# A new table of edits to the issue order of a two-layer attention and mixer kernel: the set-up and some thirty later instructions change places

## The chip, the core and the metric

The kernel runs on one core of a Trainium2 chip. The metric is device microseconds of one execution. Lower is better. The core's engines each take their own list of instructions in order and meet only through semaphores: TensorE (PE, with its weight loads PEld), ScalarE (ACT), VectorE (DVE), GpSimd (POOL), and SyncE (SP), which issues the transfers.

## The reference

The input x has 2048 rows (tokens) of 448 values. Two layers are applied, each an attention block A and a mixer block B, all with the same weights.

```python
x = x + A(layernorm(x)); x = x + B(layernorm(x))      # twice
# A: qkv = x @ wqkv, 16 heads of 28; softmax(q k^T * 28**-0.5) v; then @ wo
# B: h = gelu(layernorm(x) @ w1), shifted by rows in four column groups, @ w2; x1 = x + that
#    x1 + gelu(layernorm(x1) @ w3) @ w4
```

## The kernel before, in words

**Staging.** The rows are 16 tiles of 128. The 16 heads stand in four groups of four, and each head is padded from 28 to 32, so that one group fills 128 partitions. Keys are kept as kT (four groups by columns of tokens), queries as qT, values as vaug (token tiles by padded heads). The scores of one head and one key tile against 512 queries are one matmul with 32 rows (L1646). They go to PSUM banks 0 to 4: one ACT instruction (L1884) takes the exponentials of three banks (128x1536), the next of the two others (128x1024), in turn, and writes them to the ring PT of 15 slots. While ACT works on one set of banks, PE fills the other. The products with the values (L1042, 128x32 a piece) add up in bank 5. Banks 6 and 7 serve all other matmuls: the projections of keys, queries and values, the mixer's layers, and fillers, which are matmuls of the identity (L2377) that only keep PE at work. A part of the exponentials is computed by DVE instead (L1728 to L1762).

**Set-up.** Rows 0 to 511 are loaded, normalised on DVE (L1236, L1237, L1251, with the reciprocal root on POOL, L1244), transposed on PE in 16 pieces of 128x128 (L1275, four to a tile, each tile in a bank of its own) and copied to xT by DVE (L1282). Meanwhile ACT packs the key weights into wk_pad in four copies (L1180), squares their first 128 rows (L1192, into a slot of PT), packs two pieces of the query weights into wq_pad (L1180; POOL packs the other two, L1185) and squares their first 128 rows (L1192, into fb). PE sums the columns of these squares: four one-column matmuls for the keys and four for the queries (L1042 by the helper mm; ps<-ones_bf,PT and ps<-ones_bf,fb). DVE copies the eight sums to csum (L1204), PE adds them up by head (ps<-csum,astat), and DVE and POOL turn the two into a ratio for each head (L1206 to L1215, with a power on POOL, L1210). The first key projection (L1051 by the helper mm4; four steps ps<-xT,wk_pad over the four pieces of 128 features) goes to bank 7. ACT squares it (L1381) and adds a constant into kT (L1399); PE sums the squares by head (ps<-sq,astat), DVE takes the maximum (L1411), and from it and the ratio come the biases of the queries (L1560, L1562). With them ACT writes the first qT (L1459, from bank 5), and the first scores and exponentials can start.

**Order.** A planner in the kernel makes a list of 11,186 operations, numbered in the order in which it placed them (an operation is one instruction, or four matmuls side by side where the helper mm4 or a filler issues it). Then a method rearranges it by two tables that were written out beforehand:

```python
        for (a, b) in moves:
            p, q = prv[a], nxt[a]
            nxt[p] = q
            if q is not None:
                prv[q] = p
        for (a, b) in moves:
            q = nxt[b]
            nxt[b], prv[a], nxt[a] = a, b, q
```

MOVES holds pairs (a, b): operation a is taken out of its engine's list and put right behind operation b. WEAVE holds one letter an operation (t PE, s ACT, v DVE, g POOL, d SP) and says in which order over all engines the operations are noted. From that order each operation's waits are worked out: for data that it reads, for buffers that it overwrites. On the chip only the order within an engine and these waits count.

Of the kernel before, what the change touches and what calls it, by code (L numbers as in the profile page):

```python
# [61 lines left out]
)  # L62
WEAVE = (
    "vdvvvvsgdvgvvdtgtvgdtvtgdtsgtgvdvtvttdvtvvtdttvtvdgtgtdvtvtdtstvvtdgsvtttdtsgtttttstttsvttttvstttttgtvttstttvt",
    "tgsvtttvtttvvttttvvtvvtvtvtvtvtstgtstsvtttvvtvvtvvtsttvvtsvvtttstvttstvttvvtgtsvtttvvstvttsvttvtttsvtttvttsttv",
    "svtgvgvvtttsvttttvttttvttvdstvttttttvttsvttvttttvstvtdttvtttvtvtdsttttvtstttttdvtstvtdtttttvtttttstvdttttvvstt",
    "vtvsttttttvvtvgdtgtttsvvtttttttvtsvgtttgvtttttsvtdtttgttvtdtttsvtdttvttdtvtdstvtdvttttsvtgtttttttvtstttttgttts",
    "vttttdvstttvtgsvtttvtttttttvtdsvttdtttdtsttvttdtgtsttvttttttstvttttttgtvtstvtdtttstvttttttttgttsttttttsttvtvtg",
    "tsttvttvtttvsvttvtvttttvttstttvtsvdtttdtvtdvtttttvsdvtvtttdvsdvttvtdttdtvtsvtvdtttvvtstvtttvtttttttsttttttttts",
    "vtttvtttvstdttttvtgttstttvtttttsvtttttvstttvtttvttttsttvttttttsvttvtvtvtvtvsttvtvststtvdtttttgtttdvtstttttttvs",  # L70
    "tttttttttdtgsvtttttttsvgttttdtgdvsttdtvtgstvttttttttttsttttttsttvtttgtsttvttttttstvttgttttvstttvttdtsdttvttttt",
    "ttvsttttvtttsttvttvtvtvvtvsttttvvtsvtvttvtttttttvsttttvttsttvtvttstvtdttdtvsttttttttvtgtttstttttstttttttttttst",
    "vtttttgsvttvddsvtttdvtvtdtttsvtttttvtvvvvsvtttvtvvsvtvttvtvttvttvttvsttttvttsvttgttttvtdtsdvttttdvsttvtttttttt",
# [57 lines left out]
    "tdttvtttsvttttdttvttttttstvttttttvstvttttvttvtsttttvdsttvtdgtttttttttsttttttvsttvttvtdttttvsdttttvttttttstttvt",  # L131
    "tttttvttsdtvttttvttdtstdvtttvtdstvttdtttvstttttgttttttttstttvtttvtstttvttttttdsvttttttttvsgttdttttdvtsttvtttts",
# [18 lines left out]
    "tsttgttttvttttttdgtvttgtsvtttttttgtvstttttttgttttvtgttttgttvsttdtttvtttstvtttttttttttttsdvttttttttttttvsttttvt",  # L151
# [9 lines left out]
    "tvtgttgstvttttttvtttttttttttvdtstttgtvttttstttttvttttttttttttsvtttttttttttttvstttvtttttttsttttttsttttttttttttt",  # L161
# [2320 lines left out]
```

## Time and profile before

| what | value |
|---|---|
| median of 3 runs | 1025.42 us (1025.31 to 1028.83) |
| profiled execution, its own time | 1025.07 us |
| its span, first to last instruction | 1023.4 us |
| granted TensorE clock over the span | 1.000 |
| start of the first exponential (L1884) | 15.97 us |
| exponential of 128x1536 | x375, mean 1553 ns |
| exponential of 128x1024 | x406, mean 1130 ns |

The span is 1.7 us shorter than the profiled execution's own time. "x8" behind a line of the timeline is the number of instructions merged in it; the first column is the start, the second how long they took together. "[0.90 <-DVE bc L1562]" says that the engine stood idle for 0.90 us before, and what ended it. Where nothing holds them up, the exponentials of the trace start 1.33 us (128x1536) and 0.90 us (128x1024) after one another, less than their means: the spans shown overlap.

### The profile page before, as it was taken

How to read it: one execution, taken by the hardware profiler on the slowest of the kernel's cores; microseconds unless marked ns; L12 is line 12 of the kernel's file. 1: busy time of each engine (PE TensorE's matmuls, PEld its weight loads, DVE VectorE, ACT ScalarE, POOL GpSimd, SP SyncE). 2: the span in 40 equal slices, each digit the busy share in tenths (PEclk: the TensorE clock that was granted, in tenths of full speed). 3: DMA queues.
4: the chain of work that ended last, by engine and by line, in shares of the span. 5: the costliest groups of instructions: out<-in, count | busy, mean ns of one | idle time of the engine just before them, and what ended most of it. 6: DMA issues, size and time to landing. Idle time of an engine off the chain costs nothing.

```text
span 1023.4 us, 35818 instructions
## 1 busy us (share of the span) xinstructions
PE 969.9 (95%) x16109; PEld 408.7 (40%) x16109; DVE 813.1 (79%) x1572; ACT 981.0 (96%) x894; POOL 291.4 (28%) x462
## 2 busy tenths in 40 slices
PE   8999999999999999999999999999999999999998
PEld 4332443443333243333433443433433433444565
DVE  8877999989888958876877868688898589866651
ACT  8999999999999999999999999999999999999942
POOL 3312021531353006252425112012624120532230
PEclk9999999999999999999999999999999999999999
DMA  4643412310321014122141124423301020121101
GB/s 126 155 108 116 127 45 80 53 39 23 75 62 28 12 37 96 23 48 33 45 114 33 38 68 135 141 75 91 64 25 38 18 68 13 34 56 32 26 12 34
DMA packets 99393, 62.55 MB, mean 61 GB/s; under 512 B 68712, under 2 KB 88552, under 8 KB 99240
## 3 DMA queue, kind: packets, MB, share of 16 engines
q1 hardware_dynamic: 99240, 60.27, 23.0%
q8 instruction: 126, 2.06, 0.8%
q14 instruction: 27, 0.22, 0.1%
HBM read 28.16 MB, written 16.76 MB: 44 GB/s over the span
## 4 chain that ended last, share of the span: by engine, by line
ACT 71%; PE 23%; DVE 3%; DMA 1%; issue 1%; SPq 0%; DVEq 0%; ACTq 0%
ACT PT L1884 65%; PE ps L1051 13%; PE ps L1646 5%; PE ps L1042 4%; ACT h2T L2331 2%; ACT fb L2150 1%; PE ps L2377 1%; ACT L1884 1%; DVE h2T L2309 0%; ACT hT L2132 0%; DMA rT<-ub 0%; ACT L2331 0%; DMA PT<-in_A_wqkv_dram 0%; DMA obf<-in_A_x_dram 0%; DMA rscr<-rT 0%
## 5 line engine op out<-in xcount | busy, mean ns | idle before, releaser
L1884 ACT ACTIVATE PT<-ps 128x1024 bf16<-128x1024 f32 (+1 forms) x782 | 887.4, 1332 | 3.5 <-PE ps L1646 2.2
L1646 PE MATMUL ps<-qT,kT 32*128 32x512 bf16 (+1 forms) x2304 | 269.9, 335 | 24.2 <-ACT PT L1884 17.9
L1042 PE MATMUL ps<-PT,vaug 128*32 128x512 bf16 (+1 forms) x2420 | 245.9, 341 | 0.9 <-DVE vaug L1488 0.2
L1051 PE MATMUL ps<-xT,w 128*32 128x512 bf16 (+4 forms) x2656 | 178.1, 344 | 4.2 <-DVE h2T L2309 3.0
L1646 PEld LDWEIGHTS ps<-qT,kT 32*128 32x128 bf16 x2304 | 69.8, 91 | 256.0 <-ACT PT L1884 227.4
L2377 PE MATMUL ps<-ident 128*32 128x256 bf16 x3348 | 145.9, 277 | 2.0 <-POOL ident L1136 1.5
L1042 PEld LDWEIGHTS ps<-PT,vaug 128*32 128x32 bf16 x2420 | 74.0, 95 | 89.5 <-issue 70.9
L2377 PEld LDWEIGHTS ps<-ident 128*32 128x32 bf16 x3348 | 94.8, 97 | 28.9 <-issue 12.1
L1991 POOL TENSOR_TENSOR otn<-ub,fb 128x512 bf16<-128x512 f32 (+1 forms) x31 | 35.4, 1141 | 211.4 <-DMA fb<-rscr 211.4
L1728 DVE TENSOR_SCALAR yd<-ps 128x512 int32<-128x512 f32 x109 | 74.5, 684 | 22.5 <-PE ps L1646 21.0
L1051 PEld LDWEIGHTS ps<-xT,w 128*32 128x32 bf16 (+1 forms) x2656 | 69.5, 95 | 56.0 <-issue 22.9
L1051 PE MATMUL ps<-w,h2T 128*32 128x448 bf16 x1120 | 75.4, 355 | 4.4 <-ACT h2T L2331 4.3
L1755 DVE SCALAR_TENSOR_TENSOR fb<-yd 128x512 f32<-128x512 uint16 x109 | 79.0, 728 | 0.7
L1757 DVE SCALAR_TENSOR_TENSOR fb<-fb,yd 128x512 f32<-128x512 f32 x109 | 78.3, 721 | 0.7
L1762 DVE SCALAR_TENSOR_TENSOR PD<-yd,PD 128x512 int16<-128x512 int16 x109 | 75.0, 690 | 1.6
L2309 DVE CAST h2T<-ps 128x512 bf16<-128x512 f32 (+1 forms) x70 | 44.4, 635 | 16.0 <-PE ps L1051 14.9
L1384 POOL TENSOR_TENSOR sq<-qT 128x512 bf16<-128x512 bf16 x24 | 28.5, 1188 | 95.8 <-DVE qT L1443 93.0
L1384 POOL TENSOR_TENSOR sq<-kT 128x512 bf16<-128x512 bf16 (+2 forms) x32 | 30.3, 949 | 83.1 <-DVE kT L1398 80.0
L1759 DVE TENSOR_SCALAR PD<-fb 128x512 bf16<-128x512 f32 x109 | 51.5, 475 | 1.0
L1051 PE MATMUL ps<-xT,wk_pad 128*32 128x512 bf16 (+2 forms) x576 | 47.5, 359 | 0.9 <-issue 0.3
L1646 PE MATMUL ps<-wk_pad,kT 32*128 32x512 bf16 x256 | 39.6, 384 | 4.5 <-ACT PT L1884 4.0
L1051 PE MATMUL ps<-xT,wq_pad 128*32 128x512 bf16 x512 | 43.2, 382 | 0.1
(189 smaller groups left out, 1194.6 us busy)
## 6 DMA issues: line engine op xcount, KB each, us to landing
uscr<-ub SPq DMA_DIRECT2D x28, 256.0 KB
ub<-uscr SPq DMA_DIRECT2D x28, 256.0 KB, 6.8
fb<-rscr SPq DMA_DIRECT2D x24, 256.0 KB
xnd<-xn SPq DMA_DIRECT2D x28, 128.0 KB, 2.0
xd<-x_res SPq DMA_DIRECT2D x16, 224.0 KB, 2.2
x_res<-xd SPq DMA_DIRECT2D x16, 224.0 KB, 4.2
w<-in_B_w_dram SPq DMA_DIRECT2D x5, 448.0 KB, 6.0
obf<-in_A_x_dram SPq DMA_DIRECT2D x16, 112.0 KB
```

Of the source, the lines that this page charges most:

```text
L1042: return lambda e: e.matmul(out=out, lhsT=lhsT, rhs=rhs, start=start, stop=stop, **kw)
L1051: r.append(e.matmul(out=out[c:c + w, :], lhsT=lhsT[:, c:c + w], rhs=rhs, start=start, stop=stop, tile_position=(0, c)))
L1384: return both("sq", 0.15 + NW * 0.0018, 0.07 + NW * 0.00104, lambda e: e.tensor_tensor(out=sq[:, si, 0:NW], in0=src, in1=src, op=ALU.mult) ...
L1646: yield op("pe", (0.005 + NW * 0.00042) / nc_, lambda e, i=i, kc=kc, j=j, g=g, qt=qt, a=a, NW=NW, bank=bank: e.matmul(out=ps[:, bank, i * ...
L1728: yield op("dve", c_ps(512), lambda e: e.tensor_scalar(out=y, in0=ps[:, bi(bank), :], scalar1=SCALE * L2E * FS, scalar2=-126.0 * FS, op0=A ...
L1755: yield op(D_[0][0], D_[0][1], lambda e: e.scalar_tensor_tensor(out=q, in0=lo, scalar=E2 / E3 * FS, in1=lo, op0=ALU.add, op1=ALU.mult), re ...
L1757: yield op(D_[1][0], D_[1][1], lambda e: e.scalar_tensor_tensor(out=q, in0=q, scalar=E1 / E3 * FS * FS, in1=lo, op0=ALU.add, op1=ALU.mult) ...
L1759: yield op(D_[2][0], D_[2][1], lambda e: e.tensor_scalar(out=pdt, in0=q, scalar1=E3 / FS ** 3, scalar2=E0, op0=ALU.mult, op1=ALU.add), rea ...
L1762: yield op(D_[3][0], D_[3][1], lambda e: e.scalar_tensor_tensor(out=pdt.bitcast(I16), in0=hi, scalar=128.0, in1=pdt.bitcast(I16), op0=ALU. ...
L1884: yield op("act", 0.069 + n * w * 0.000833, lambda e, bk=bk, s0=s0, n=n, w=w: e.activation(out=PT[:, s0:s0 + n, 0:w], in_=ps[:, bk[0]:bk[0 ...
L2309: ev = op("dve", c_ps(m * NW), lambda e, hr=hr, pv=pv: e.tensor_copy(out=hr, in_=pv), reads=[("ps", bi(b))], writes=hk, touch=[b])
L2377: return [e.matmul(out=ps[32 * c:32 * c + 32, bi(b), 0:256].rearrange("p (a n) -> p a n", n=128), lhsT=ident[:, 32 * c:32 * c + 32], rhs=i ...
```

## The change

Forty-one pairs are added to MOVES and six taken out; WEAVE is adapted. No operation is added or taken away, and no operation computes anything else. The lists of SP and POOL keep their order. The core of the diff, with all added pairs in whole lines of it:

```diff
@@ -17,60 +17,64 @@
...
-    (241, 247), (243, 241), (274, 285), (276, 274), (555, 550), (572, 568), (574, 572), (564, 575), (565, 564),
-    (595, 587), (597, 595), (604, 638), (605, 604), (606, 605), (652, 648), (657, 655), (756, 745), (758, 756),
...
+    (94, 115), (95, 94), (96, 95), (97, 96), (125, 118), (128, 125), (130, 134), (238, 231), (244, 238), (245, 244),
+    (246, 245), (247, 246), (261, 266), (262, 261), (274, 285), (276, 274), (555, 550), (572, 568), (574, 572),
+    (564, 575), (565, 564), (595, 587), (597, 595), (599, 597), (601, 599), (603, 601), (604, 634), (605, 604),
+    (606, 605), (645, 606), (646, 645), (647, 646), (648, 647), (652, 643), (657, 655), (756, 745), (758, 756),
+    (759, 758), (856, 850), (857, 856), (858, 857), (930, 935), (931, 930), (937, 931), (913, 941), (916, 913),
+    (966, 951), (964, 981), (965, 964), (975, 987), (1024, 1018), (1026, 1024), (1031, 1026), (991, 1031),
...
+    (7286, 7288), (7300, 7306), (7301, 7300), (7302, 7309), (7338, 7334), (7500, 7488), (7472, 7493), (7473, 7472),
...
-    (9616, 9627), (9680, 9672), (9681, 9680), (9682, 9681), (9684, 9682), (9697, 9689), (9699, 9697), (9700, 9699),
...
+    (9616, 9626), (9627, 9642), (9680, 9672), (9681, 9680), (9682, 9681), (9684, 9682), (9697, 9689), (9699, 9697),
...
+    (10134, 10128), (10135, 10134), (10597, 10591), (10675, 10653), (10676, 10675), (10677, 10676), (10683, 10663),
...
+    (11181, 11180), (107, 92), (4484, 4523), (5925, 5889), (6339, 6324), (7096, 7213), (8003, 7983), (8678, 8674),
+    (242, 232), (560, 593), (727, 732), (746, 762), (914, 904), (912, 907), (1033, 1011), (1041, 1037), (1453, 1431),
...
+    (5678, 5657), (5912, 5878), (5951, 5905), (6131, 6120), (6329, 6322), (6473, 6500), (7298, 7283), (7393, 7379),
+    (7406, 7393), (7434, 7390), (7466, 7424), (7450, 7445), (7791, 7769), (7991, 7973), (8016, 7987), (8032, 8016),
...
 WEAVE = (
-    "vdvvvvsgdvgvvdtgtvgdtvtgdtsgtgvdvtvttdvtvvtdttvtvdgtgtdvtvtdtstvvtdgsvtttdtsgtttttstttsvttttvstttttgtvttstttvt",
...
+    "vdvvvvsgdvgvvdtgtvgdtvtgdtsgtgvdvtvttdvtvvtdttvtvdgtgtdvtvtdtstvvtdgsvtttdtsgtttttstttsvttttvstgtttttttvtttttt",
...
```

In words, with the planner's numbers:

- Set-up, PE: the four column sums of the key weights (94 to 97) stood after the first transpose of the third tile (91) and ahead of the seven last transposes (99 to 108); now they stand behind the third of six fillers that follow the transposes (115). The first two steps of the key projection (125, 128) move ahead of the four column sums of the query weights (119 to 123). The sum by head (130, ps<-csum,astat) moves from between the second and third step of the key projection to behind the fourth (134).
- Set-up, ACT: the square of the query weights (107) moves ahead of the second copy into wq_pad (93).
- Near 23 to 26 us of the trace, PE: the last step of a value projection (238) and four products with the values (244 to 247) move ahead of three score matmuls (233 to 235) and a sum of key squares (237); three scores (264 to 266) move ahead of two steps of a query projection (261, 262). DVE: the copy of the second value tile (242) moves up by two places.
- Near 55 to 63 us: three scores (599, 601, 603) move ahead of five products with the values; two scores (640, 641) and two steps of a value projection (638, 643) move behind four products (645 to 648); a bias on DVE (560) moves back by seven places.
- Near 90 to 100 us, PE: two steps of a key projection (913, 916) move back by 19 places, past seven scores; two products (964, 965) back by ten; one step of a key projection (991) back by 18.
- Near 683 to 692 us: two products (7472, 7473) move back by some 15 places, one step of a query projection (7500) up by seven, and on DVE a step of its own exponentials (7393, L1759) up by three, another (7466, L1755) up by four, and the last step of a query group (7450, L1472) up by one.
- Near 885 us: the product 9627 moves back past six mixer steps (9616 to 9642) and six scores. Near 963 us: the product 10683 moves up by eleven.

More of the change, by code (lines that the diff above doesn't have):

```diff
@@ L45 @@
     (9149, 9148), (9150, 9149), (9317, 9307), (9312, 9339), (9313, 9312), (9315, 9313), (9316, 9315), (9414, 9403),
[16 rows of a table removed]
[17 rows of a table added]
 )
 WEAVE = (
-    "vdvvvvsgdvgvvdtgtvgdtvtgdtsgtgvdvtvttdvtvvtdttvtvdgtgtdvtvtdtstvvtdgsvtttdtsgtttttstttsvttttvstttttgtvttstttvt",
-    "tgsvtttvtttvvttttvvtvvtvtvtvtvtstgtstsvtttvvtvvtvvtsttvvtsvvtttstvttstvttvvtgtsvtttvvstvttsvttvtttsvtttvttsttv",
-    "svtgvgvvtttsvttttvttttvttvdstvttttttvttsvttvttttvstvtdttvtttvtvtdsttttvtstttttdvtstvtdtttttvtttttstvdttttvvstt",
-    "vtvsttttttvvtvgdtgtttsvvtttttttvtsvgtttgvtttttsvtdtttgttvtdtttsvtdttvttdtvtdstvtdvttttsvtgtttttttvtstttttgttts",
+    "vdvvvvsgdvgvvdtgtvgdtvtgdtsgtgvdvtvttdvtvvtdttvtvdgtgtdvtvtdtstvvtdgsvtttdtsgtttttstttsvttttvstgtttttttvtttttt",
+    "ttttvgssvvttttttttvvvvvvtvvvtvtstgtstsvtttvvtvvtvvtsttvvtsvvtttstvttstvttvvtgtsvtttvvstvttsvttvtttsvtttvttsttv",
+    "svtgvgvvtttstvtttttvtttstvttvttvtdttttsvtvttvttsvttvtdttvtttvttvdstttttvstttttdvtstvtdtttttvtttttstvdttttvvstt",
+    "vtsvttttttvvtvgtdtgttsvvtttttttvtsvtgttgvtttttsvttdttgttvttdttsvtdttvttdtvtdstvtdvttttsvtgtttttttvtstttttgttts",
     "vttttdvstttvtgsvtttvtttttttvtdsvttdtttdtsttvttdtgtsttvttttttstvttttttgtvtstvtdtttstvttttttttgttsttttttsttvtvtg",
-    "tsttvttvtttvsvttvtvttttvttstttvtsvdtttdtvtdvtttttvsdvtvtttdvsdvttvtdttdtvtsvtvdtttvvtstvtttvtttttttsttttttttts",
-    "vtttvtttvstdttttvtgttstttvtttttsvtttttvstttvtttvttttsttvttttttsvttvtvtvtvtvsttvtvststtvdtttttgtttdvtstttttttvs",
+    "tsttvttvtttvstvttvttttvttstttvtsvdtttdtvtvdvvsdvtvtttdttttvtsdvttvtdttdtvtsvtvdtttvtvtsttttvtttvttttstttttttts",
+    "vtttvtttvstdttttvtgtttstvttttttsvtttttvstttvtttvttttsttvttttttsvtvttvtvtvvtsttvtvststtvdtttttgtttdvtstttttttvs",
     "tttttttttdtgsvtttttttsvgttttdtgdvsttdtvtgstvttttttttttsttttttsttvtttgtsttvttttttstvttgttttvstttvttdtsdttvttttt",
-    "ttvsttttvtttsttvttvtvtvvtvsttttvvtsvtvttvtttttttvsttttvttsttvtvttstvtdttdtvsttttttttvtgtttstttttstttttttttttst",
-    "vtttttgsvttvddsvtttdvtvtdtttsvtttttvtvvvvsvtttvtvvsvtvttvtvttvttvttvsttttvttsvttgttttvtdtsdvttttdvsttvtttttttt",
+    "ttvsttttvtttsttvttvtvtvvtvstttvvsvtvttvtttttttvsttttvttsttvtttvttstvttdttdvsttttttttvtgttsttttstttttttttttsttt",
+    "vtttvstgttvddsvtdtvttvdttttsvttttvtvttvvvsvtttvtvvsvtvttvtvttvttvttvsttttvttsvttgttttvtdtsdvttttdvsttvtttttttt",
     "tvttsvttdvttvvtvtdvsvttvdttvtttttdttttvsttsttvsttttttvttsttttvttvtttsvttttvtttsttttttvttttttttvtsttttvtttstvtt",
@@ L130 @@
     "vttttttvgttttdtstttdtvtttsttttvtttttdvtvsttttvttttstttttttvtttttvsttttvtttsvtttvdtttttstttvtttttsvttttvgttvdst",
-    "tdttvtttsvttttdttvttttttstvttttttvstvttttvttvtsttttvdsttvtdgtttttttttsttttttvsttvttvtdttttvsdttttvttttttstttvt",
-    "tttttvttsdtvttttvttdtstdvtttvtdstvttdtttvstttttgttttttttstttvtttvtstttvttttttdsvttttttttvsgttdttttdvtsttvtttts",
+    "tdttvtttsvttttvdttttttvttstttvttttsvttvttttvttstttvtdsdvttgttttttttttsvttttttvsttvtttttvttvsdttttvttdttstttttt",
+    "vttttdtvsttvtdttttttdstttvtttvdstvttdtttvstttttgttttttttstttvttttvstttvttttttdsvttttttttvsgttdttttdvtsttvtttts",
     "vdgtttvtdttsttvttttttsttgtttttttsttvttsvgttttttttvtstvtttttsdvttttttvttsvtttvtdttsttvtvttsvdtttttvdtstttvttttv",
@@ L150 @@
     "ttttgttvtgtvsttttgtttttdtvgsgtttvtttgtvtttgtstdvtttttttgvgttsvttttdtttgttttvttttttttttttgtsvtttttttdgtttvttttt",
-    "tsttgttttvttttttdgtvttgtsvtttttttgtvstttttttgttttvtgttttgttvsttdtttvtttstvtttttttttttttsdvttttttttttttvsttttvt",
+    "tsttgttttvttttttdgtvttgtsvtttttttgtvstttttttgttttvtgtttgttvsttdtttvtttstvttttttttttttttsdvttttttttttttvsttttvt",
     "ttttttvttsttttvttttttttttstvtvtttdtgtttttstttttttvttttttttttttstvttvttttttvtttttvtttvtdtvttttttvtttttvttttdttv",
@@ L160 @@
     "tdvtttttttttttttstttttttttttttstvtttttvtttsvtvttttgttgvttttttsttttttvtttttttttstttvtttttvsttttvttdgtttvtvtsttt",
-    "tvtgttgstvttttttvtttttttttttvdtstttgtvttttstttttvttttttttttttsvtttttttttttttvstttvtttttttsttttttsttttttttttttt",
+    "tvtgtttgstvttttttvttttttttttvdtsttttgvttttstttttvttttttttttttsvtttttttttttttvstttvtttttttstttttttstttttttttttt",
     "tttvttttttttvstttttvtttsttttvtttttvtttttvttttsvtttttvtttsttvtvtgttgttsgtttttgttvstgtvttgttttgtttgttgvttvgtgtgt",
```

64 rows, old and new, of the table MOVES are left out of this document.

## The prediction

> **What bounds the kernel now.** First the page: busy shares, and the chain of work that ended last.
>
> ```profile
> PE 969.9 (95%) x16109; PEld 408.7 (40%) x16109; DVE 813.1 (79%) x1572; ACT 981.0 (96%) x894; POOL 291.4 (28%) x462
> ACT 71%; PE 23%; DVE 3%; DMA 1%; issue 1%; SPq 0%; DVEq 0%; ACTq 0%
> ```
>
> ACT is idle for 42 us in all. Next, what ACT waited for, from the first exponential to the start of the tail (16 to 970 us):
>
> ```profile
> ACT PT L1884 <- PE ps L1646: 2.2, 4, 0.7
> ACT fb L2150 <- DVE fb L2149: 0.8, 1, 0.8
> ACT PT L1884 <- PE ps L1042: 0.3, 1, 0.3
> ```
>
> The columns are the total, the number of waits, the longest. Only 3.3 us in 954 are real waits. So an edit in this stretch can gain little, and the time before the first exponential counts in full, because an unbroken ACT list moves with it. The timeline of the set-up:
>
> ```profile
> 8.15 0.61 ACT L1192 ACTIVATE PT<-wk_pad 128x512 bf16<-128x512 bf16 x1
> 8.82 0.25 PE L1042 MATMUL ps<-ones_bf,PT 128*128 128x1 bf16 x4 [0.66 <-ACT PT L1192]
> 8.94 0.55 PE L1275 MATMUL ps<-ident,xn 128*128 128x128 bf16 x7
> 9.30 0.76 DVE L1282 COPY xT<-ps 128x512 bf16<-128x512 bf16 x2 [0.76 <-PE ps L1275]
> 9.61 0.61 ACT L1192 ACTIVATE fb<-wq_pad 128x512 bf16<-128x512 bf16 x1
> 10.46 0.61 PE L1051 MATMUL ps<-xT,wk_pad 128*32 128x512 bf16 x8
> 11.12 0.61 PE L1051 MATMUL ps<-xT,wk_pad 128*32 128x512 bf16 x8
> 11.79 0.60 ACT L1381 ACTIVATE sq<-ps 128x512 bf16<-128x512 f32 x1 [1.56 <-PE ps L1051]
> 12.97 0.69 DVE L1411 TENSOR_REDUCE kmaxc<-ps 128x1 f32<-128x512 f32 x1 [1.01 <-PE ps L1051]
> 14.34 0.78 ACT L1459 ACTIVATE qT<-ps,bc,rcol 128x512 bf16<-128x512 f32 x1 [0.90 <-DVE bc L1562]
> 15.97 2.37 ACT L1884 ACTIVATE PT<-ps 128x1536 bf16<-128x1536 f32 x2
> ```
>
> Seven ready transposes stand behind column sums that wait 0.66 us for ACT; DVE waits 0.76 us for them, and the delay goes down the key chain to the exponential. Last, PE's waits (24 to 105 us) and its fillers, from windows restricted to the identity:
>
> ```profile
> PEld ps L1646 <- ACT PT L1884: 25.1, 61, 1.1
> PE ps L1646 <- ACT PT L1884: 2.1, 5, 0.8
> 45.00:55.00 10.00, 0.00 (x0) 0.00 (x0) 0.00 (x0) 0.00 (x0) 1.00 0.44 118
> ```
>
> There is not one filler from 45 to 95 us: PE has no spare work to drop there. Its waits are for banks that ACT still reads. PE and ACT bound this stretch together, and what counts is by how much both move.
>
> **The change part by part.** The sum is made against the profiled execution, 1025.07 us (span 1023.4 and 1.7 around it). The median is 0.35 above it.
>
> Set-up. The first transpose of the third tile starts at 7.93 and the others follow it 0.055 apart, where they now start at 8.94. The third tile's last starts at 8.10, not 9.05. The trace has 0.255 from that start to DVE's copy, so 8.35; but DVE's earlier two copies started at 7.79 and 8.13 and copies follow 0.34 apart, so the third copy starts at 8.46 and the fourth at 8.80, ending at 9.22 instead of 10.06. Three fillers fit before the moved sums, which still start at 8.82 with the ACT square; three more fillers of 0.11 and the mode change of 0.15 end near 9.39. There the key projection starts, 1.07 earlier than 10.46.
>
> Its first two steps take 0.23 each, to 9.84. The query sums then need ACT's query square. That square now follows the copy that it reads, so it can't overlap it: the trace has such a pair at L1163 and L1165 (end 3.51, next start 3.54), against 0.095 of overlap between independent copies. It starts at 9.235 + 0.03 and ends 0.61 later, at 9.88, instead of 10.22. The sums start at 9.94 (0.06 behind, as at 8.82), last 0.18 to the next step, and steps three and four start at 10.12 and 10.35. The fourth ends 0.39 later, at 10.74, against 11.73: 0.99 gained. The sum by head follows at 10.66 instead of 11.01 and holds the query projection by 0.11, which starts at 10.78 (before 11.56). Four steps of 0.216 and 0.1 later the key squares are summed at 11.74 instead of 12.53. This is the narrowest place: 0.78 gained. DVE's maximum follows 0.45 later, at 12.19.
>
> The other branch: csum can be copied at 10.23 instead of 10.57; the ratio's chain then keeps its own distances (0.88 to wsum, 0.60 to POOL's power, 1.01 for it) and ends at 12.71 instead of 13.05. DVE needs it at 12.80. It is late next, by a margin of 0.09: a slip of POOL beyond that comes off the gain. The second copy into wq_pad ends at 10.35 instead of 9.70; the query projection hides it until 10.78. Bias, first qT, scores and the first exponential keep their distances: **15.97 becomes 15.19, minus 0.78**. Bounds: nothing, if the ratio's branch slips by as much (the 0.34 that it gains stands against it, so 0.34 at least if rows hold), and 0.99, the gain at the projection.
>
> Products ahead of scores (23 to 26 us). The exponential at 24.14 waited 0.31 for products still reading PT slots that it overwrites; it began 0.52 later than its pair allows. With the products first, PE issues them at 22.88 and the scores at 23.20, in time. The scores at 26.14, held by two query steps from 25.60, move ahead of them: their bank is free at about 25.65. ACT could gain 0.52 + 0.18. PE, however, saves only what it idled: the operation behind both groups (26.46) comes at 26.19, so 0.27. The next exponentials start as their scores end, and after 45 us there is nothing to drop. I take **minus 0.27**, the PE figure, and keep 0.70 as the other end. The moved value copy on DVE starts as soon as its projection ends, 0.8 earlier, and passes a normalisation of 0.39 and a small statistic; those feed a store that is not awaited here.
>
> 55 to 100 us. Scores 599 to 603 would start at 58.38, but their banks are read until 58.67 and the next start after such an end is 0.06 later: PE idles 0.35 before them, where five products stood; the exponential behind them had 0.20 to spare and starts the same. Scores 640 and 641 come 0.16 later against 0.42 to spare. Scores 917 and 919 meet banks read until 90.92: 0.6 of idling in place of two key steps, which return behind 941 and push the next scores by 0.19, against 0.17 to spare. Products 964 and 965 then fill two idle column groups beside 983 and 984 instead of a round of their own (about 0.2 back). The moved key steps are read by DVE at 95.24 and now end near 94.5: no wait. **Zero**, between minus 0.15 (the one late start here, at 97.61) and plus 1.3 (0.35 + 0.6 + 0.16 + 0.19, all lost).
>
> 683 to 692 us: exponentials follow at their closest throughout, with fillers beside them; hidden by ACT. 885 us: the exponential at 887.03 is 1.05 late, but because the mixer step 9616 waits until 885.61 for transfers (L1261), which moving one product past it does not hasten; the product costs the scores at 887.45 some 0.1 against 0.48 to spare. 963 us: ACT is dense. Zero each, at best minus 1.05 for the second.
>
> Waits: working the reads and writes out in both orders, one differs: the exponential at 24.14 waits for the last score in place of a product, whichever is last in PE's order. No wait is added, and no transfer changes place in SP's or POOL's list.
>
> Sum: -0.78 - 0.27 = **-1.05**: 1024.02 on the profiled scale, 1024.4 as a median.
>
> **The rivals.**
>
> *More is kept* (0.17). ACT's losses at the edited places go too: 0.78 + 0.52 + 0.18 + 0.15 + 1.05 = 2.68, so 1022.7. For: ACT is the chain's main engine. Against: no filler from 45 us, and 9616's transfer.
>
> *Given back* (0.16). The stretch without fillers eats the gain, or the ratio's branch sets the bias: 1025.2 to 1025.6. The early exponentials then wait for scores, as four do already.
>
> *Pulled-ahead scores stop PE* (0.13), the slower side. If PE is the bound at 59 and 91 us, waiting for banks with ready work behind is lost: the whole 1.3, and the 0.27 cannot be kept. That gives 1025.42 - 0.78 + 1.3 = 1025.9. It turns the sign once the stalls exceed 1.05. Against: the exponentials there have 0.2 to 0.5 to spare.
>
> *PE's clock* (0.04), slower too. Granted clock is 1.00 in every stretch of the set-up, although PE is busy only 1.34 of 2.00 us from 8 to 10. Were the 28 projection matmuls on the chain (11.19, 1.76 us) run at half speed, they would add 1.76: 1026.1. [...]
>
> *Changes nothing in order* is excluded: an executed list differs where the tables do.
>
> **How the numbers follow.** Forecast 0.50, rivals 0.17, 0.16, 0.13, 0.04. About 0.5%, or 5.1 us, is what a measurement of this kernel can tell from no change, and no case gets there: all edited places' losses together are half of it. The same program's three runs spread by 3.4 us, though, and the chain passes transfers (3.46 us at 259.58, 3.42 at 731.53) whose meeting with other traffic a shift may alter; I leave 0.06 for faster and 0.06 for slower out of the cases' edges, 0.88 within. The range covers the forecast with its bounds, *more is kept* and the slower rivals to some spread: 1022.2 to 1026.6.
>
> **What would show it.** The seven transposes at 8.0 to 8.3; the key projection at 9.4; the maximum near 12.2; the first exponential at 15.2; no wait of ACT on L1042 at 24; at 105 us ACT about 1 us ahead, kept to the tail. I am wrong on the set-up if the first exponential is later than 15.5, on the PE bound if ACT is over 1.5 ahead at 105 us, and as a whole if the tail starts over 2 us away from its old place less 1.05.

## The result, and the profile after

The changed kernel's median is 1024.57 us (22 runs, 1023.0 to 1027.61), the kernel before's beside it 1026.48 us (22 runs): ratio 0.9984, 95% interval 0.9976 to 0.9992, so by the ratio 1.64 us less (0.82 to 2.46). In a second comparison it had 1024.37 us (12 runs) against 1025.92 us (29 runs): 0.9991, interval 0.9981 to 1.0001, which alone does not tell it from no change. Its profiled execution took 1025.44 us with a span of 1023.6 us at a granted clock of 1.000. That span is 0.2 us longer than the profiled span of before, although the medians go the other way; much of what follows is about that.

In the changed file every line number past the table is 4 higher (L1884 is now L1888). The page's busy shares and its chain of work that ended last:

```profile
PE 968.4 (95%) x16107; PEld 408.1 (40%) x16109; DVE 814.0 (80%) x1572; ACT 981.7 (96%) x894; POOL 293.5 (29%) x462
ACT 70%; PE 24%; DVE 3%; DMA 1%; issue 1%; SPq 0%; DVEq 0%
```

No engine's load changed: it is the same work in another order, and ACT still bounds it. The timeline of the set-up (start, duration, engine, line, operation):

```profile
7.75 1.41 DVE L1286 COPY xT<-ps 128x512 bf16<-128x512 bf16 x4
7.89 0.62 PE L1279 MATMUL ps<-ident,xn 128*128 128x128 bf16 x8
7.96 0.61 ACT L1196 ACTIVATE PT<-wk_pad 128x512 bf16<-128x512 bf16 x1
8.89 0.25 PE L1046 MATMUL ps<-ones_bf,PT 128*128 128x1 bf16 x4
9.13 0.63 ACT L1196 ACTIVATE fb<-wq_pad 128x512 bf16<-128x512 bf16 x1
9.41 0.60 PE L1055 MATMUL ps<-xT,wk_pad 128*32 128x512 bf16 x8
9.94 0.25 PE L1046 MATMUL ps<-ones_bf,fb 128*128 128x1 bf16 x4
10.79 0.60 ACT L1385 ACTIVATE sq<-ps 128x512 bf16<-128x512 f32 x1 [0.57 <-PE ps L1055]
12.10 0.69 DVE L1415 TENSOR_REDUCE kmaxc<-ps 128x1 f32<-128x512 f32 x1 [0.48 <-PE ps L1055]
13.52 0.78 ACT L1463 ACTIVATE qT<-ps,bc,rcol 128x512 bf16<-128x512 f32 x1 [1.04 <-PE ps L1055]
15.15 2.38 ACT L1888 ACTIVATE PT<-ps 128x1536 bf16<-128x1536 f32 x2
```

All eight transposes now run in one go, and DVE's four copies with them; before, seven transposes and two copies stood behind sums that waited 0.66 us for ACT. The first exponential starts at 15.15 us instead of 15.97. What ACT waited for from 16 to 970 us (total, number, longest):

```profile
ACT PT L1888 <- PE ps L1650: 2.9, 5, 1.1
ACT fb L2154 <- DVE fb L2153: 1.1, 1, 1.1
```

The wait for products (L1042 before) is gone, as the change meant. But the waits for scores total 2.9 us instead of 2.2, and those for DVE 1.1 instead of 0.8. Some of the early lead was lost later in this execution; the experiments ask whether the change did that. Last, PE's waits from 24 to 105 us and the stretch without fillers:

```profile
PEld ps L1650 <- ACT PT L1888: 25.3, 59, 0.9
PE ps L1650 <- ACT PT L1888: 2.7, 9, 0.6
45.00:55.00 10.00, 0.00 (x0) 0.00 (x0) 0.00 (x0) 0.00 (x0) 1.00 0.39 105
```

PE waits for ACT's banks about as long as before (25.3 and 2.7 us for 25.1 and 2.1), and still has no filler to drop.

### The profile page after: what moved, and what is told of

The parts are those of the page before. It is cut to its first block, busy times and chain, and to the rows that moved or that the text cites. A ratio compares the mean times of both kernels' runs of the same rounds, so it can differ in the third digit from the quotient of the medians.

```text
span 1023.6 us, 35818 instructions
## 1 busy us (share of the span) xinstructions
PE 968.4 (95%) x16107; PEld 408.1 (40%) x16109; DVE 814.0 (80%) x1572; ACT 981.7 (96%) x894; POOL 293.5 (29%) x462
## 4 chain that ended last, share of the span: by engine, by line
ACT 70%; PE 24%; DVE 3%; DMA 1%; issue 1%; SPq 0%; DVEq 0%
ACT PT L1888 64%; PE ps L1055 14%; PE ps L1650 5%; PE ps L1046 4%; ACT h2T L2335 2%; PE ps L2381 1%; ACT fb L2154 1%; ACT L1888 1%; ACT hT L2136 0%; DMA rT<-ub 0%; DVE h2T L2313 0%; ACT L2335 0%; DMA obf<-in_A_x_dram 0%; DMA rscr<-rT 0%; DVE PD L1766 0%
## 5 line engine op out<-in xcount | busy, mean ns | idle before, releaser
L1888 ACT ACTIVATE PT<-ps 128x1024 bf16<-128x1024 f32 (+1 forms) x782 | 887.2, 1328 | 3.7 <-PE ps L1650 2.9
L1759 DVE SCALAR_TENSOR_TENSOR fb<-yd 128x512 f32<-128x512 uint16 x109 | 78.3, 722 | 0.8
```

What stands on the lines that cost most here:

```text
L1759: yield op(D_[0][0], D_[0][1], lambda e: e.scalar_tensor_tensor(out=q, in0=lo, scalar=E2 / E3 * FS, in1=lo, op0=ALU.add, op1=ALU.mult), re ...
L1888: yield op("act", 0.069 + n * w * 0.000833, lambda e, bk=bk, s0=s0, n=n, w=w: e.activation(out=PT[:, s0:s0 + n, 0:w], in_=ps[:, bk[0]:bk[0 ...
```

## The experiments

Twelve more profiles of the table's variants can be laid over one another, since all kernels have the same operations. I call *lead* the start of an ACT instruction less the start of the same one in the first profile of before (negative is earlier; the median over a stretch), and *w* the start of ACT's first copy of the key weights into wk_pad. Diffs show the pairs of MOVES; WEAVE follows from them. Line numbers shift by a few with the length of each variant's table (L1192 of before is L1193 in s1 and s3). **Theory A**: the edits act where they stand, what they bring adds up, and what happens past 105 us is scatter between executions. Its rivals are in each expectation.

**Both kernels again** (no edit), one execution each.

> The kernel before, profiled once more, as a control. Between the two profiles shown, the changed kernel's lead over the kernel before grows to 1.14 us by 110 us and then shrinks in five steps (near 176, 237, 743, 753 and 887 us) to a lag of 0.29. Theory A: the steps are the scatter of transfers and of phases between executions; this profile then differs from the first one of the same kernel by steps of 0.2 to 0.5 us, at some of these places or others, and the first exponential starts within 0.15 us of 15.97. Theory B: the edits cause the steps; then the two profiles of the kernel before agree within 0.15 us all along.

> The changed kernel, profiled once more. Both theories: first exponential at 15.15, within 0.15; lead over the kernel before 1.1 to 1.5 us at 110 us. Theory A (scatter): the five later steps do not all return at the same places, and the span lies 0.5 to 2 us below 1023.6. Theory B (caused by the edits): the same five steps return, and the lead ends within 0.4 us of nothing.

Measured: 1024.04 us (before, span 1022.3) and 1024.71 us (after, span 1023.0). The kernel before differs from its own first profile by -0.30 us up to 100 us, +0.20 at 110 to 150, +0.60 at 245 and -1.03 past 890. Its first exponential came at 15.67, which misses the 0.15 that I had allowed. The changed kernel repeats itself to 0.01 us up to 150 us and then parts from itself by up to 0.9 us. By itself the changed kernel's repeat does not decide: its span is 0.6 us lower, as theory A has it, but of the five steps four come back, three with other sizes (0.92, 0.19 and 0.68 us for 0.24, 0.40 and 0.29) and the one near 887 us alike (0.36 for 0.35), and the lead ends at -0.35, within the 0.4 of theory B. Against B stand the control, which parts from itself by as much, and a third profile of the changed kernel (the timed one below), which gains 0.22 at 176 us and ends at -0.84. So a lead of under 1 us past 105 us is no evidence from one execution. The largest step of all is in neither expectation: at 866 us every other profile, before again included, gains 0.93 us on the first profiles of before and after.

**The set-up's edits alone, and all the others alone.**

```diff
 # e3_setup_only, against before
+    (94, 115), (95, 94), (96, 95), (97, 96), (125, 118), (128, 125), (130, 134), (107, 92),
 # e4_rest_only: every other pair of the change, without these eight
```

> Only the edits of the set-up (column sums, key projection, square ahead of copy); the order from 20 us on is that of the kernel before. Theory A: first exponential at 15.15 to 15.2; the exponential that stood at 24.14 stands at 23.3 with its wait of 0.3 us still there, and the lead is 0.8 at 30 us and 0.75 to 0.85 at 110 us, since every engine's list moves together: 0.8 us faster as a whole, a ratio near 0.9992. Rival (given back): the stretch without fillers from 45 to 95 us takes it back and the lead at 110 us is under 0.4.

> All edits but those of the set-up. Theory A: first exponential at 15.97; the one at 24.14 starts 0.5 us earlier, the one at 26.57 0.7 earlier, of which 0.2 to 0.25 is given back by 28 us as PE's next scores are late; lead 0.3 to 0.45 at 110 us: ratio near 0.9996. Rival (PE stops at the scores pulled ahead near 59 and 91 us): over 0.3 is lost there and the lead at 110 us is below 0.1 or a lag. Rival (more is kept): a lead of 0.7 or more at 110 us, and another 0.3 to 1.0 won near 887 us.

Measured: 1024.95 us (11 runs), ratio 0.9992 (0.9981 to 1.0003), and 1024.82 us (11 runs), ratio 0.9992 (0.9983 to 1.0001); neither ratio tells them from no change. The leads do:

| lead, us | 16 | 24.14 | 26.57 | 28–58 | 64–88 | 110–150 | 890–970 |
|---|---|---|---|---|---|---|---|
| e3, set-up alone | -0.78 | -0.78 | -0.78 | -0.78 | -0.78 | -0.77 | -0.33 |
| e4, the rest alone | +0.02 | -0.47 | -0.64 | -0.40 | -0.29 | -0.31 | -1.94 |
| after (and again) | -0.82 | -1.30 | -1.48 | -1.23 | -1.12 | -1.14 | +0.27 (-0.35) |

Up to 150 us the parts add: -0.77 and -0.31 make -1.08, and both together measure -1.14, the 0.04 between the two set-ups included. Past 150 us the lead does not follow the edits: of the three, the change with the smallest lead at 150 us ends with the largest.

**The set-up, edit by edit.**

```diff
 # s1_cols_back: the key weights' column sums behind the transposes
+    (94, 115), (95, 94), (96, 95), (97, 96),
 # s2_cols_back_keys: s1, and the key projection ahead of the query sums
+    (125, 118), (128, 125), (130, 134),
 # s3_squares_ahead: only ACT's query square ahead of the copy
+    (107, 92),
 # s3b_squares_fills: s3, and three fillers ahead of the column sums
+    (113, 91), (114, 113), (115, 114),
```

> One part of the set-up's edits alone: the four column sums of the key weights' squares (94 to 97) moved behind the transposes, everything else as in the kernel before. Let w be the start of ACT's first copy of the key weights; in the kernel before the first exponential starts at w + 9.70 (6.27 and 15.97, 5.98 and 15.67, 6.29 and 15.99). Theory A (PE takes its queue in order and the query weights' column sums stand ahead of the key projection, so the ACT square of the query weights sets the start): third copy to xT at 8.4 instead of 9.3, query sums and key projection where they were (w + 4.01 and w + 4.19), first exponential at w + 9.70 within 0.05: nothing gained. Theory B (each of the three edits brings its share of the 0.78): first exponential 0.2 to 0.3 earlier, w + 9.4 to 9.5. Theory C (the whole gain is the transposes', the other two edits ride along): 15.2, whatever w is.

> Two of the three edits: column sums behind the transposes, and the key projection's first steps ahead of the query weights' column sums (the PE order of the set-up is that of the changed kernel); ACT keeps its order, with the second copy of the query weights ahead of their squares. Theory A: first key projection at 9.4 as in the changed kernel, query sums still at w + 4.01 (10.28 for w = 6.27), key projection's end and csum 0.34 later than in the changed kernel, first exponential at w + 9.2, 15.49 for w = 6.27 and 15.2 for w = 5.98; so 0.48 of the set-up's gain. Theory C (the order on PE is all that counts): 15.15 to 15.2 whatever w is.

> The third edit alone: ACT squares the query weights ahead of their second copy; PE keeps its order. Theory A: query sums 0.34 earlier, at w + 3.67 or 9.94, whichever is later, key projection 0.34 earlier at about 10.1, first exponential at w + 9.36 (15.63 for w = 6.27), so 0.34 gained where the transposes' edit alone gains nothing. Theory C: first exponential at w + 9.70, nothing gained, since the transposes stand where they stood.

One execution each gave 1025.81 (s1), 1024.78 (s2) and 1025.35 us (s3), beside 1026.37 for the kernel before; single times that scatter by more than they differ. Starts of the steps, worked out of each trace by the order of its instructions:

| us | w | key projection | query sums | maximum | first exponential | less w |
|---|---|---|---|---|---|---|
| before | 6.27 | 10.46 | 10.28 | 12.97 | 15.97 | 9.70 |
| before again | 5.98 | 10.16 | 9.98 | 12.68 | 15.67 | 9.69 |
| s1 | 6.08 | 10.26 | 10.08 | 12.78 | 15.78 | 9.70 |
| s3 | 6.35 | 10.45 | 10.27 | 12.96 | 15.96 | 9.61 |
| s3b | 6.07 | 10.19 | 9.94 | 12.71 | 15.70 | 9.63 |
| s2 | 6.38 | 9.73 | 10.38 | 12.54 | 15.59 | 9.21 |
| after | 6.07 | 9.41 | 9.94 | 12.10 | 15.15 | 9.08 |
| set-up alone | 6.25 | 9.41 | 9.98 | 12.14 | 15.19 | 8.94 |
| after, timed | 6.56 | 9.63 | 10.30 | 12.45 | 15.50 | 8.94 |

s1 came out as theory A says: the third copy to xT is 0.9 us earlier (8.40) and nothing is gained, w + 9.70. s2 too, w + 9.21 for 9.2. (x was normalised 0.32 us later there, so its key projection is at 9.73; the query sums still set the end.) s3 missed: 0.09 gained, where I expected 0.34. PE's timelines tell why; first s1, then s3:

```profile
9.05 0.51 PE L2378 MATMUL ps<-ident 128*32 128x256 bf16 x12
10.08 0.25 PE L1043 MATMUL ps<-ones_bf,fb 128*128 128x1 bf16 x4 [0.52 <-ACT fb L1193]
```

```profile
8.90 0.25 PE L1043 MATMUL ps<-ones_bf,PT 128*128 128x1 bf16 x4 [0.74 <-ACT PT L1193]
9.02 0.55 PE L1276 MATMUL ps<-ident,xn 128*128 128x128 bf16 x7
9.50 0.84 PE L2378 MATMUL ps<-ident 128*32 128x256 bf16 x24
10.27 0.25 PE L1043 MATMUL ps<-ones_bf,fb 128*128 128x1 bf16 x4
```

With the transposes moved, PE idles 0.52 us for ACT's query square. With the square moved, PE has no pause: transposes and 24 fillers reach to the query sums by themselves. In the kernel before the two ended together (the square at 10.22, the fillers at 10.26), so that either edit alone meets the other's wait, and it takes both (or s2's detour around the query sums) to gain. s3b was to show it by taking fillers away as well:

> The third edit alone, as in s3 (ACT squares the query weights ahead of their second copy), and PE's fills 113 to 115 (matmuls on the identity whose result nothing reads, 12 instructions, 0.42 us) moved ahead of the key weights' column sums, where PE waits 0.66 to 0.74 us for ACT. w is again the start of ACT's first copy of the key weights. Theory D (in the kernel before, two things let the query sums start at w + 4.01, ACT's square of the query weights and PE's own queue of transposes and fills, and they end within 0.1 us of each other, so that an edit of one alone gains nothing): now both are out of the way, query sums at w + 3.65 to 3.75, key projection at w + 3.85 to 3.95, first exponential at w + 9.35 to 9.45. Rival (s3's miss came of something else on PE, such as the fourth copy to xT, which ended at w + 3.7 there): first exponential at w + 9.61 as in s3.

Measured: 1026.51 us, first exponential at w + 9.63, the rival's number. It is inconclusive: in this execution PE was already late ahead of the edit. The first eight transposes, s3b and then s3:

```profile
6.32 1.03 PE L1276 MATMUL ps<-ident,xn 128*128 128x128 bf16 x8
```

```profile
6.31 0.70 PE L1276 MATMUL ps<-ident,xn 128*128 128x128 bf16 x8 [0.28 <-DVE xn L1252]
```

In s3b they start some 0.105 us apart, in s3 some 0.055. The clock records of the two traces grant PE full clock from 7.39 us in s3b and from 5.75 us in s3. The third tile's first transpose came at 8.30 instead of 7.94, and so the column sums at 8.91 followed three fillers rather than ACT. The query sums came at w + 3.87, 0.05 before s3's, but the fourth copy to xT (from 9.73) then set the key projection. So the two tied waits are read from s1 and s3, and their joint removal only from the full set-up edits.

**Without the moves at 55 to 63 us.**

```diff
 # no_55, against after
-    (560, 593), (599, 597), (601, 599), (603, 601), (604, 634), (645, 606), (646, 645), (647, 646), (648, 647), (652, 643),
+    (604, 638), (652, 648),
```

> The changed kernel without its moves at 55 to 63 us (the scores 599 to 603, the projection steps and fills 604 to 606 and 645 to 648, 560 on DVE: the old order there). Theory A (these moves, priced at zero, cost the 0.11 us that ACT's lead loses between 52 and 64 us): same start as the changed kernel (first exponential 15.15 to 15.2), ACT's lead over the kernel before's first profile -1.23 at 52 us and still -1.23 to -1.25 at 64 to 100 us, where the changed kernel has -1.12. Rival (the 0.11 is lost to a place that comes late there whatever the order): -1.12 at 64 to 100 us again. After 107 us scatter between executions, up to 0.6 us, as in the runs so far; time 1024.0 to 1025.5.

> The changed kernel without its moves at 55 to 63 us, timed. One execution of it gave 1022.47 us, 3.9 less than the kernel before beside it. Theory A (the early lead of -1.14 plus 0.11 is what the edits bring, and what follows 107 us is scatter): 1.0 to 2.0 us less than the kernel before, ratio 0.998 to 0.999, 0.1 to 0.3 less than the changed kernel, within both intervals; lead at 64 to 100 us -1.13 to -1.25. Rival (the moves at 55 to 63 us set where the later places at 230, 270 and 870 us fall, and without them these are won): 3 to 4 us less than the kernel before, ratio 0.9961 to 0.9971.

> The changed kernel again, timed on the same chip as the two beside it. Theory A: ratio 0.998 to 0.999 to the kernel before, first exponential at 15.15 to 15.3, lead at 64 to 100 us -1.12 counted from a first exponential 0.82 early, less by what the key weights or x come late.

One execution gave 1022.47 us; timed, the same kernel has 1025.28 us (12 runs), ratio 0.9994 (0.9983 to 1.0004). The first was a lucky execution, and the rival with 3 to 4 us falls; the time itself is above what I expected of theory A, with an interval that holds it. The changed kernel beside it came to 0.9991, just past what I expected, and its first exponential to 15.50 instead of 15.15 to 15.3: its key weights came late (w 6.56). The leads settle the question that the experiment was for:

| lead, us | 16 | 28–58 | 64–88 | loss between |
|---|---|---|---|---|
| after | -0.82 | -1.23 | -1.12 | 0.11 |
| after, timed | -0.46 | -0.88 | -0.77 | 0.11 |
| e4, the rest alone | +0.02 | -0.40 | -0.29 | 0.11 |
| no_55 | -0.71 | -1.12 | -1.13 | none |
| no_55, timed | -0.84 | -1.25 | -1.26 | none |

PE's waits from 55 to 65 us, in the changed kernel, and then without these moves (as before the change):

```profile
PE ps L1650 <- ACT PT L1888: 0.5, 2, 0.3
```

```profile
PE ps L1650 <- ACT PT L1888: 0.2, 1, 0.2
```

A second wait of 0.3 us for a bank that ACT still reads stands where five products stood. All the moves at 55 to 63 us were taken back together, so the 0.11 is shown for them as a whole; that this wait is what costs it is argued.

**Going on in the same direction.**

```diff
 # earlier_still, against no_55
+    (116, 143), (117, 116), (129, 124), (131, 129), (144, 138),
```

> A version that goes on where the edits stop, from the changed kernel without its moves at 55 to 63 us: two of PE's fills (116 and 117, 0.28 us) moved from ahead of the key projection to behind the query projection, the key heads' sum (144) ahead of two steps of the query projection, and DVE's two clearings of the wv and astatq tiles moved from between csum and wsum to where DVE idles ahead of csum. Theory A: key projection at 9.2, query sums at 9.75, csum at 10.04, POOL's half power from 11.3 to 12.3, maximum at 11.7 to 12.4, first exponential at 14.8; ACT's lead at 64 to 100 us -1.5 to -1.6; ratio to the kernel before 0.9980 to 0.9988. Rival (another wait is right behind: the query projection's last steps or the transfers that ACT's copies of 24 to 28 us need): first exponential 15.0 to 15.15, lead -1.2 to -1.3, ratio 0.9985 to 0.9992.

Measured: 1024.61 us (12 runs), ratio 0.9991 (0.9982 to 1.0000): no better than the changed kernel. The steps came as worked out (key projection 9.18, query sums 9.78, maximum 11.81, POOL's power 11.38), and then the gain went: first exponential 15.24, lead -1.15 at 64 to 88 us. That is later than either theory had it. ACT's timeline shows the rival's wait:

```profile
13.33 0.78 ACT L1463 ACTIVATE qT<-ps,bc,rcol 128x512 bf16<-128x512 f32 x1 [0.48 <-PE ps L1456]
15.24 2.36 ACT L1888 ACTIVATE PT<-ps 128x1536 bf16<-128x1536 f32 x2
```

The bias is ready at 13.09, but qT now waits for the query projection's own norm (L1456), whose input I had pushed back by putting the key heads' sum ahead of two of its steps. The query side stood right behind the key side.

## Why the prediction held, point by point

**The set-up, -0.78**: measured between -0.71 and -0.84 in five executions with these edits, and -0.46 in a sixth (the timed one). Its steps: copies to xT at 8.42 and 8.75 (8.46 and 8.80 predicted), key projection 9.41 (9.39), query sums 9.94 (9.94), query projection 10.78 (10.78), key heads' sum 11.66 (11.74), maximum 12.10 (12.19), POOL's end 12.71 (12.71), first exponential 15.15 (15.19). That the query sums agree to the hundredth is partly luck: ACT's query square ended at 9.76 there, not 9.88, and the sums stood behind PE's own two key steps, which end as predicted. In e3, with the key weights as late as before (w 6.25), the square ends at 9.93, the sums start at 9.98 behind it and the first exponential at 15.19, as worked out. The ratio's branch did come next: DVE's step behind it starts at 12.75, 0.04 after POOL and as the maximum ends. What I had not seen is that the old start hangs on a transfer. ACT's first copies, with what they waited for, in before and in before again (in the changed kernel's timed profile they start at 6.56, after 1.17 us of waiting for the same transfer):

```profile
6.27 1.98 ACT L1180 ACTIVATE wk_pad<-PT 128x448 bf16<-128x448 bf16 x4 [0.90 <-DMA PT<-in_A_wqkv_dram]
```

```profile
5.98 1.98 ACT L1180 ACTIVATE wk_pad<-PT 128x448 bf16<-128x448 bf16 x4 [0.60 <-DMA PT<-in_A_wqkv_dram]
```

Before, the first exponential follows this landing at 9.70. After, it follows at 8.94 if the weights come late and stands at 15.15 if they come early, since then x's own chain sets it. The gain is therefore 0.76 for a late landing and 0.52 (15.67 less 15.15) for the earliest seen; 0.78 was right because the profiled execution of before was of the late kind, which was luck.

**Products ahead of scores, -0.27, other end -0.70**: the size was off. In e4 ACT gains 0.49 at 24.14 us and 0.18 more at 26.57 (0.02 of its start counted), 0.67 in all, which is nearly the ACT figure, and gives 0.25 back by 28.4 us: 0.42 kept. PE's operation behind both groups came 0.39 earlier (26.07 for 26.46), not 0.27. The reason I gave, that PE's figure and not ACT's is what stays, holds; that figure was 0.12 too small, and what makes up the difference was not traced.

**55 to 100 us, zero, between -0.15 and +1.3**: +0.11 at 63 to 66 us, shown by leaving the moves at 55 to 63 us out, and -0.05 at 97.61. The 0.35 of PE's idling ahead of scores 599 to 603 was not wholly covered by the exponential's spare time; the 0.6 before 917 and 919 was (lead -1.12 on both sides).

**683 to 692, 885 and 963 us, zero each**: nothing can be told from no change. In e4 the lead is -0.55 at 670 us and -0.53 at 730. At 887 us after loses 0.35, and its other two profiles 0.36 and 0.33, but so does the kernel that has only the set-up's edits (0.41), and e4, which has the edit there, gains 0.71. The kernel before, profiled again, gains 0.74 there without any edit.

**The sum, -1.05**: measured -1.14 at 110 to 150 us, since the 0.15 too little at 24 to 28 us and the 0.11 too much nearly cancel, which is luck. So is part of the agreement: the lead counts from a profile whose key weights came late, and from before again, where they came early, it is 0.82 at 64 to 88 us. By the ratios the two comparisons give -1.64 and -0.92 (by the second's interval anything from -1.95 to +0.1), which hold it.

**"Kept to the tail"** failed for the profiled execution: -0.47 at 730 us, +0.27 past 890. The chain that ended last, before, and then after, near 731 us:

```profile
731.53 3.42 DMA rscr<-rT
735.62 4.30 DMA rT<-ub
```

```profile
731.04 3.58 DMA rscr<-rT
735.29 4.56 DMA rT<-ub
```

The first transfer is issued 0.49 us earlier and lasts 0.16 longer, the next 0.26 longer: 0.42 of the lead is spent on two transfers. In the repeated profile and in the timed one, neither transfer is on the chain at all. So this step is the unknown for which the prediction kept its spread, not a price of the change. The steps near 176, 237 and 887 us (0.24, 0.40 and 0.35 lost) were not traced to a cause.

**The rivals.** *More is kept*: ACT's 0.67 at 24 to 27 us was there, but 0.25 of it was given back by 28.4; 9616's 1.05 was not won by the edit, since after and its repeat lose 0.35 at that place. *Given back*: a tenth of it (0.11 of 1.2), at 63 to 66 us. *Pulled-ahead scores stop PE*: moves at 55 to 63 us cost 0.11 instead of 1.3. *PE's clock*: by after's clock record it did not fall within the set-up (1.00 from 4.43 us to the end of the span), but PE does not have full clock from the start either, although the profile's column reads 1.00 there. The fillers of 256 columns take 0.21 us for four at first and 0.11 later, and the traces' clock records grant full clock from a time that differs by execution: 4.43 us in after, 6.11 in before, 7.39 in s3b. In s3b (7.39) and no_55 (6.80) this reaches the first eight transposes, which take 1.03 and 0.89 us instead of 0.70. The 1.76 us that the rival adds for projections at half speed is shown by no run: the first two steps of the key projection took 0.60 us in after and 0.61 in before. A granted clock of 0.50 came later in the kernel, in the profiles of s2, before again and s3b (below), and 15 of the changed kernel's 34 runs have a mean below 1.000. **Signs**: transposes, key projection, maximum, first exponential and the vanished wait at 24 us all as listed.

## What to carry to other kernels

Where an engine's list stands still for a moment, look for every wait that would end at the same time as the one you remove: in s1 and s3 each edit alone gave 0 and 0.09 us, and all of them together 0.76. A time gained ahead of an engine that is 96% busy was kept here to 150 us; past that, transfers on the chain (0.42 us in after) and stretches at a granted clock of 0.50 (0.50 us in s2, 1.46 in s3b) moved single executions by as much. Judge an edit worth 1 us by the starts of the same instructions in two traces, in the stretch that repeats itself, and not by medians of a dozen runs, whose intervals here are 2 us wide.

## What the runs showed of the hardware that was not expected

The scatter of the times goes with the clock. Over the runs for which the clock is listed, the kernel before had a median of 1025.13 us at a granted clock of 1.000 (19 runs), 1026.08 at 0.998 (17), 1026.90 at 0.997 (9) and about 1027.3 below (6). s2's profile has 0.998, and its windows show where it comes from (PE, PEld, DVE, ACT, POOL busy with counts, then granted clock, DMA share, GB/s):

```profile
100.72:104.13 3.41, 2.25 (x24) 0.61 (x24) 3.23 (x17) 3.41 (x5) 0.00 (x0) 1.00 0.71 220
104.13:107.54 3.41, 3.37 (x25) 0.75 (x25) 2.32 (x7) 3.02 (x3) 0.91 (x1) 0.50 0.01 2
```

One stretch of 3.41 us at a granted clock of 0.50, which loses 1.7 of 1023 us of clock, the 0.998; the lead falls by 0.50 there. The repeated profile of before has such a stretch at 104.3 to 107.7 us (0.50 lost), and s3b one at 369.2 to 372.6 us, which cost it 1.46. Ahead of each, PE was busy for only a part of the time: 2.25 of 3.41 us in s2 (66%), 2.57 of 4.00 in before again (64%, from 100 to 104 us) and 1.44 of 3.40 in s3b (42%, from 365.90 to 369.30), with pauses for banks of 0.76, 0.63 and 0.30 us in s2 and one of 1.96 for ACT's h2T in s3b. But the busy share alone does not decide. In s3, PE was busy for 2.13 us from 100.72 to 104.13, less than in s2, and the granted clock was 1.00 there and from 104 to 108 us; the first profile of before has 2.12 us and 1.00. s2 itself has a stretch with PE busy for 43% near 367 us, and its one stretch at 0.50, near 104 us, makes up its whole 0.998. First s3, then s2:

```profile
100.72:104.13 3.41, 2.13 (x24) 0.61 (x24) 3.25 (x14) 3.41 (x4) 0.14 (x1) 1.00 0.68 207
```

```profile
366.96:370.37 3.41, 1.46 (x32) 0.88 (x36) 0.00 (x0) 3.38 (x3) 0.00 (x0) 1.00 0.11 41
```

The kernel before lost the clock near 104 us in one profile and kept it in the other, with PE busy for 2.57 and 2.62 us from 100 to 104 us. What decides is not shown.

At full clock alone the changed kernel's median is 1024.07 us (19 of 34 runs), before's 1025.13 (19 of 51): 1.06 less (0.2 to 1.6 when the runs are drawn again and again), the early lead's size; the runs are pooled here over several comparisons. Whether the change also makes such stretches rarer (15 of 34 runs below 1.000, against 32 of 51) stays open: no profile of the changed kernel has one.
